# A new order table and new engine choices for a one-core attention and gated feed-forward kernel, with tiles handed out by first release

## The chip, the cores and the metric

The kernel runs on one core of a Trainium2 chip. The metric is the device time of one execution in microseconds (us). A core has five engines with queues of their own: TensorE (PE in the rows; PEld is its weight load), VectorE (DVE), ScalarE (ACT), GpSimd (POOL) and SyncE (SP), which here only issues DMA transfers. Each engine executes its instructions in the order in which they were written, and an instruction waits until the semaphores that it names are set.

## The reference

Inputs are q, k, v of 4 batches, 8 heads, 768 positions and 64 elements per head, 8 memory keys and values per head, and the weights of the feed-forward block.

```python
# attention: chunks of 32 queries see 16 positions to the left, the chunk, 8 to the right, and 8 memory slots
scores = scale * np.matmul(q_c, k_full.transpose(0, 1, 3, 2))
scores = scores - np.max(scores, axis=-1, keepdims=True)
a = np.exp(scores)
a = a / (np.sum(a, axis=-1, keepdims=True) + 1e-09)
out[:, :, c_start:c_end] = np.matmul(a, v_full)
# feed-forward: x is the attention output, 512 wide
h = np.maximum(x @ w_in, 0.0)                   # 512 -> 1024
for k in range(3):
    conv_out += conv_w[k] * hp[:, k:k + S, :]   # along the positions, per channel
gate = 1.0 / (1.0 + np.exp(-conv_out))
out = (h * gate) @ w_out                        # 1024 -> 512
```

## The kernel before, in words

**Attention.** The 4 batches are cut into halves (hf) of 384 positions and head pairs (cc, 4 of them), which makes 32 steps. A step's score matmuls (L310, tile `s`, in PSUM, one buffer) are reduced to their maximum on VectorE (L267), which is subtracted on VectorE and put through exp on ScalarE (L269, L270) or taken as the bias of exp on ScalarE (L283). The result stands in one of two tiles `e0`, `e1`; VectorE sums it (L290) and takes the reciprocal (L293), and VectorE or GpSimd multiplies by it (L294). TensorE transposes the tile (L325, PSUM tile `t`, one buffer), ScalarE copies it out (L327, `w_t`), TensorE multiplies by the values (L334, into the same `t`), and the result is split into a high and a low part, `x_hi` on ScalarE (L340) and `x_lo` on VectorE (L341). The first four steps are done singly, the others in pairs, so that there are 18 groups, named below by their number.

**Feed-forward.** Every product is three matmuls: high by high, high by low, low by high. `w_in` and `w_out` arrive as 64-bit numbers in 16 loads of 512 KB (L208), 8 for each, and are split on the engines into a high and a low part (L212 to L238). The letter of `W_IN` and `W_OUT` says which engines do it for each of the 8 slices: C and M use a copy on ScalarE (L219) and a product (L230, L232); R and S use an addition on GpSimd (L234), a cast on ScalarE (L236) and a subtraction on GpSimd (L238). A small letter puts one step, L214, on GpSimd. `conv_w` (24 KB) arrives in the same buffer as the last slice of `w_in` (L210). `ffn_in` (L358) makes 12 matmuls for a slice fc of the 1024 hidden channels and a half of a batch, three for each head pair; `relu` (L366), the three-tap convolution (L374 or L376, then L378 twice), the sigmoid (L379), the product (L381) and the split into `g` high and low (L387, L388) follow; `ffn_out` (L402) makes 24 matmuls for 128 positions, then a copy (L405) and a store (L406).

**The order.** Nothing is scheduled at build time. Every piece of work is put into a list by `plan.op` (L111) with what it reads and writes; `Plan.run` (L143) then emits the pieces in the order of the table `ORDER`, which therefore sets the order of the instructions on each engine and of the transfers in SyncE's queue. The strings `TAP`, `MULT`, `LO`, `SOFT`, `NORM` choose an engine for one instruction of each group or slice (A ScalarE, V VectorE, G GpSimd; in `SOFT`, A and B are the two forms without the subtraction). A tile belongs to a ring with a fixed number of buffers: four for the loads of weights (`w64`), two for `k_t`, three for `q_d` and `v_t`, four PSUM banks `f`, one `s`, one `t`. A load whose ring has no free buffer waits in SyncE's queue, and all that stands behind it waits too.

The lines of the changed kernel are three to five higher than those of the rows below: L310 became L314, L325 L329, L334 L338, L358 L362, L341 L345, L208 L213, L301 L305, L234 L239, L236 L241, L219 L224, L283 L287, L405 L409.

## Time and profile before

| what | us |
|---|---|
| median of 3 runs | 352.35 (352.2 to 353.53) |
| profiled execution, whole time | 352.37 |
| its span, first to last instruction | 350.6 |
| whole time less span | 1.77 |
| TensorE busy in the span | 334.1 (95%) |
| VectorE, ScalarE, GpSimd busy | 233.1, 191.9, 83.6 |

The profiled execution is within 0.02 us of the median. "Busy" is the union of an engine's instructions. A row of a timeline gives the start, the time from the first start to the last end of a run of like instructions, the engine, line and operation, the tiles as output<-input, and how long the engine had been idle before, with what ended the idle time.

### The profile page before, as it was taken

The numbers are of one execution on the slowest core, as the hardware profiler recorded it, in microseconds if no ns is written. First come the engines' busy times: TensorE is split into PE (matmuls) and PEld (weight loads), VectorE is DVE, ScalarE is ACT, GpSimd is POOL, SyncE is SP. The second block draws the span as 40 slices with busy tenths as digits, with TensorE's granted clock in tenths as the row PEclk, the third lists the DMA queues.
The fourth block names the chain that finished last, engine by engine and source line by source line (L and its number), as shares of the span: only waits on it lengthen the run. The fifth ranks groups of instructions, "written<-read, shape, count | busy, mean of one in ns | idle before, by whom it ended". The sixth has DMA issues, their size and how long they took to land.

```text
span 350.6 us, 10290 instructions
## 1 busy us (share of the span) xinstructions
PE 334.1 (95%) x4536; PEld 297.1 (85%) x4536; DVE 233.1 (66%) x325; ACT 191.9 (55%) x314; POOL 83.6 (24%) x127
## 2 busy tenths in 40 slices
PE   1589999999999999999999999999999999999996
PEld 0468999989999998887888999998888988998885
DVE  4977998999989997989974143286840332678300
ACT  4434785877687869379842323456743352545311
POOL 1464245124473154111020000402200012121200
PEclk9999999999999999999999999999999999999999
DMA  7966979667677244022401600001212000100022
GB/s 261 391 216 204 314 249 333 230 208 228 200 206 251 66 154 148 27 93 75 125 20 36 243 0 32 0 2 60 65 45 93 30 1 2 60 0 2 0 105 76
DMA packets 19916, 42.49 MB, mean 121 GB/s; under 512 B 2336, under 2 KB 10784, under 8 KB 19872
## 3 DMA queue, kind: packets, MB, share of 16 engines
q1 hardware_dynamic: 19872, 41.85, 35.6%
q8 instruction: 35, 0.57, 0.7%
q14 instruction: 9, 0.07, 0.1%
HBM read 35.55 MB, written 6.29 MB: 119 GB/s over the span
## 4 chain that ended last, share of the span: by engine, by line
PE 85%; DVE 9%; DMA 3%; issue 1%; ACT 0%; POOL 0%; DVEq 0%; ACTq 0%; POOLq 0%
PE f L402 38%; PE f L358 34%; PE t L334 6%; PE s L310 4%; PE t L325 3%; DMA w<-in_w_out_dram 2%; DVE c L378 1%; DMA w<-in_w_in_dram 1%; DVE w_top L217 1%; DVE e L269 1%; DVE top L267 1%; DVE w_top L214 1%; DVE w L223 1%; DVE w_top L216 1%; DVE w L221 1%
## 5 line engine op out<-in xcount | busy, mean ns | idle before, releaser
L402 PE MATMUL f<-w_out_hi,g 128*128 128x512 f32 (+1 forms) x400 | 127.3, 387 | 0.0
L358 PE MATMUL f<-x_hi,w_in_hi 128*128 128x384 f32 x256 | 90.3, 353 | 0.0
L402 PEld LDWEIGHTS f<-w_out_hi,g 128*128 128x128 f32 x400 | 74.1, 188 | 15.2 <-ACT o_sb L405 0.2
L358 PE MATMUL f<-x_lo,w_in_hi 128*128 128x384 f32 x256 | 86.7, 339 | 0.0
L358 PE MATMUL f<-x_hi,w_in_lo 128*128 128x384 f32 x256 | 86.7, 339 | 0.0
L402 PE MATMUL f<-w_out_lo,g 128*128 128x512 f32 (+1 forms) x200 | 77.0, 385 | 0.0
L378 DVE SCALAR_TENSOR_TENSOR c<-h,cw,c 128x768 f32<-128x768 f32 x48 | 49.2, 1044 | 18.6 <-ACT c L374 17.4
L358 PEld LDWEIGHTS f<-x_hi,w_in_hi 128*128 128x128 f32 x256 | 48.6, 190 | 2.7 <-issue 0.2
L358 PEld LDWEIGHTS f<-x_hi,w_in_lo 128*128 128x128 f32 x256 | 48.8, 190 | 1.0
L358 PEld LDWEIGHTS f<-x_lo,w_in_hi 128*128 128x128 f32 x256 | 48.5, 190 | 0.0
L402 PEld LDWEIGHTS f<-w_out_lo,g 128*128 128x128 f32 x200 | 37.6, 188 | 6.6
L405 ACT COPY o_sb<-f 128x512 f32<-128x512 f32 (+1 forms) x25 | 14.2, 573 | 43.4 <-PE f L402 41.3
L379 ACT ACTIVATE c<-c 128x768 f32<-128x768 f32 x32 | 26.9, 847 | 19.6 <-DVE c L378 19.5
L366 ACT ACTIVATE h<-f 128x384 f32<-128x384 f32 x48 | 22.6, 490 | 26.3 <-PE f L358 26.3
L388 POOL TENSOR_TENSOR g<-c,g 128x768 fp32r<-128x768 f32 x8 | 15.4, 1925 | 70.9 <-PE f L402 35.2
L334 PEld LDWEIGHTS t<-w_t,v_t 64*64 64x64 f32 x1536 | 25.2, 140 | 4.6 <-issue 3.3
L334 PE MATMUL t<-w_t,v_t 64*64 64x32 f32 x1536 | 27.2, 224 | 0.1
L387 ACT CAST g<-c 128x768 fp32r<-128x768 f32 x24 | 19.8, 833 | 12.6 <-POOL c L381 7.1
L376 DVE TENSOR_SCALAR c<-h,cw 128x768 f32<-128x768 f32 x14 | 8.6, 617 | 26.3 <-ACT h L366 23.6
L388 DVE TENSOR_TENSOR g<-c,g 128x768 fp32r<-128x768 f32 x16 | 17.3, 1086 | 11.2 <-ACT g L387 11.0
L381 POOL TENSOR_TENSOR c<-c,h 128x768 f32<-128x768 f32 x5 | 8.9, 1781 | 63.4 <-ACT c L379 63.4
L341 DVE TENSOR_TENSOR x_lo<-t,x_hi 128x768 fp32r<-128x768 f32 (+1 forms) x18 | 15.5, 859 | 12.6 <-ACT x_hi L340 12.6
(68 smaller groups left out, 408.5 us busy)
## 6 DMA issues: line engine op xcount, KB each, us to landing
v_t<-in_v_dram SPq DMA_DIRECT2D x32, 384.0 KB, 4.4
k_t<-in_k_dram SPq DMA_DIRECT2D x28, 252.0 KB, 3.9
out_dram<-o_sb SPq DMA_DIRECT2D x23, 256.0 KB, 2.0
q_d<-in_q_dram SPq DMA_DIRECT2D x28, 192.0 KB, 4.4
w<-in_w_in_dram SPq DMA_DIRECT2D x8, 512.0 KB, 6.2
w<-in_w_out_dram SPq DMA_DIRECT2D x8, 512.0 KB, 5.3
h<-in_k_dram SPq DMA_DIRECT2D x4, 252.0 KB, 6.1
h<-in_q_dram SPq DMA_DIRECT2D x4, 192.0 KB, 5.8
```

Of the source, the lines that this page charges most:

```text
L310: nc.tensor.matmul(s.t[w * CH:(w + 1) * CH, h ^ w & 1, (i * NG + g) * KW:(i * NG + g + 1) * KW], lhsT=q_d.t[r, c], rhs=k_t.t[r, c * STEP:c ...
L325: nc.tensor.transpose(out=t.t[:, j, g * P:(g + 1) * P], in_=e.t[:, i, 1:1 + 2 * KW], identity=ident)
L334: nc.tensor.matmul(t.t[h * D:(h + 1) * D, c & 1, c // 2 * CH:(c // 2 + 1) * CH], lhsT=vs[i].t[r, o], rhs=w_t.t[r, i, o], start=True, stop= ...
L341: plan.op(lambda: nc.vector.tensor_tensor(out=lo(), in0=sums(), in1=hi().bitcast(F32), op=ALU.subtract), (t, *keys(x_hi)), keys(x_lo))
L358: nc.tensor.matmul(f.t[:, :TW], lhsT=w_in_p[c][:, fc, cc], rhs=x_p[a].t[:, cc], start=cc == 0 and i == 0, stop=cc == NCC - 1 and i == 2)
L366: nc.scalar.activation(h.t[:, 1 + o:1 + o + TW], f.t[:, :TW], AF.Relu)
L378: plan.op(lambda i=i: nc.vector.scalar_tensor_tensor(out=c.t, in0=h.t[:, i:i + S], scalar=w[i], in1=c.t, op0=ALU.mult, op1=ALU.add), (*H, ...
L379: plan.op(lambda: nc.scalar.activation(c.t, c.t, AF.Sigmoid), (c,), (c,))
L387: plan.op(lambda: nc.scalar.copy(out=g_hi(), in_=x()), (h,), (p[0],))
L388: plan.op(lambda: (nc.vector if lo == 'V' else nc.gpsimd).tensor_tensor(out=g_lo(), in0=x(), in1=g_hi().bitcast(F32), op=ALU.subtract), (h ...
L402: nc.tensor.matmul(ps.t[:, :n], lhsT=g[fc][a].t[:, tt * P:(tt + 1) * P], rhs=w_out_p[c][:, fc, o:o + n], start=fc == 0 and i == 0, stop=fc ...
L405: plan.op(lambda: nc.scalar.copy(out=o_sb.t[:, :n], in_=ps.t[:, :n]), (ps,), (o_sb,))
```

## The change

All numbers of `ORDER` are new, and most of the strings of engine choices differ in a few letters. `Plan.run` no longer demands that the tile handed out longest ago is free: it demands that some tile of the ring is free (`left` counts the readers that a tile still has). The tiles `e0` and `e1`, which were handed out in turn, are now kept in a list from which the one released first is taken.

```diff
-W_IN, W_OUT = ('CSSRMSCr', 'CMCRRSRM')
-TAP = 'AAAAAAAAVAVAVVVAVAVAVVAAVVAAVVAV'
-MULT = 'VVVGVVGVVVVVGGGVGVVVVGVVVGGGVVVV'
-LO = 'VVVVGGGVVVVVVVVVGVVVGVVVVGVVGVGV'
-SOFT = 'VVVVVAAVVAVBVVVBVBVVVAVVVVAVVBAA'
-NORM = 'GGVGGGVVGGGGGVGGVVGGVVVVVVVGVGVG'
+W_IN, W_OUT = ('CrSRMSCs', 'CCMSMRRM')
+TAP = 'AAVAAAAAAVAAAAAAVAVAVAVVAAAVVVVV'
+MULT = 'VGGVVGVVVVVGVVVVGVVVVVVGVGVVGGVV'
+LO = 'VVVGGVVVVGVVGVGGVGVGVVVVGVGVVVGV'
+SOFT = 'VVVVVAAVVAVBVVVBVBVVAAVVVVAVBBVA'
+NORM = 'GGGVGGGVVGGGGVGGVVGGGVVVVVVGVGGG'
...
 ORDER = (
-    64, 65, 1, 0, 3, 75, 17, 16, 85, 70, 33, 32, 66, 67, 18, 68, 69, 2, 71, 72, 73, 74, 4, 76, 190, 49, 5, 6, 19, 77,
...
+    64, 0, 1, 75, 49, 17, 16, 70, 65, 32, 71, 86, 33, 66, 73, 67, 68, 72, 2, 3, 74, 4, 48, 76, 5, 194, 77, 6, 139, 81,
...
-        self.rings, self.parts = ({}, defaultdict(list))
+        self.rings, self.parts, self.freed = ({}, defaultdict(list), {})
...
-                    assert len(used) < size or not used[-size].left, i
+                    assert sum((y.left > 0 for y in used)) < size, i
...
             do()
+            for x in tiles:
+                if not x.left and x.ring in self.freed:
+                    self.freed[x.ring].append(x.t)
...
+    plan.ring('e', len(e_of))
+    plan.freed['e'] = e_of
...
-        plan.ring('e', len(e_of))
-        e = Tile('e', lambda: e_of[len(plan.rings['e'][1]) % len(e_of)])
+        e = Tile('e', lambda: plan.freed['e'].pop(0))
```

TensorE near the start of the program, before: the transposes of the second group (`t_276`), the scores of the fourth (`s_285`), the values of the second, three feed-forward matmuls of slice 0 (`f_346`), and the scores of the fifth group in two halves (`s_359`).

```order
L325 MATMUL t_276<-ident_66,e1_73 128x128 x3
L310 MATMUL s_285<-h_144,h_183 32x64 x24
L334 MATMUL t_276<-w_t_311,v_t_128 64x32 x24
L358 MATMUL f_346<-x_hi0_270,w_in_hi_75 128x384
L358 MATMUL f_346<-x_hi0_270,w_in_lo_76 128x384
L358 MATMUL f_346<-x_lo0_273,w_in_hi_75 128x384
L310 MATMUL s_359<-k_t_234,q_d_181 32x64 x24
L310 MATMUL s_359<-k_t_187,q_d_142 32x64 x24
L358 MATMUL f_411<-x_hi0_270,w_in_hi_75 128x384
```

And now, from the same transposes on:

```order
L329 MATMUL t_276<-ident_66,e1_73 128x128 x3
L362 MATMUL f_283<-x_hi0_269,w_in_hi_75 128x384
L362 MATMUL f_283<-x_hi0_269,w_in_lo_76 128x384
L362 MATMUL f_283<-x_lo0_273,w_in_hi_75 128x384
L314 MATMUL s_296<-h_88,h_139 32x64 x24
L338 MATMUL t_276<-w_t_291,v_t_232 64x32 x24
L314 MATMUL s_354<-k_t_193,q_d_144 32x64 x24
L314 MATMUL s_354<-k_t_198,q_d_154 32x64 x24
L329 MATMUL t_419<-ident_66,e0_71 128x128 x3
```

The same six blocks stand between the transposes `t_276` and the end of the fifth group's scores; the three feed-forward matmuls moved from fourth to first place among those behind the transposes.

SyncE's queue, before, from its twelfth to its twenty-third load (`w64` is a slice of `w_in`, or `conv_w`):

```order
L301 DMA q_d_142<-in_q_dram 128x384
L301 DMA h_144<-in_k_dram 128x504
L301 DMA q_d_181<-in_q_dram 128x384
L301 DMA h_183<-in_q_dram 128x384
L301 DMA q_d_185<-in_q_dram 128x384
L301 DMA k_t_187<-in_k_dram 128x504
L208 DMA w64_228<-in_w_in_dram 128x1024
L301 DMA k_t_234<-in_k_dram 128x504
L301 DMA v_t_263<-in_v_dram 128x768
L301 DMA v_t_350<-in_v_dram 128x768
L208 DMA w64_353<-in_w_in_dram 128x1024
L301 DMA k_t_415<-in_k_dram 128x504
```

And now:

```order
L305 DMA h_139<-in_q_dram 128x384
L305 DMA q_d_144<-in_q_dram 128x384
L215 DMA w64_148<-in_conv_w_dram 128x48
L305 DMA q_d_154<-in_q_dram 128x384
L305 DMA q_d_183<-in_q_dram 128x384
L305 DMA k_t_193<-in_k_dram 128x504
L305 DMA k_t_198<-in_k_dram 128x504
L305 DMA v_t_232<-in_v_dram 128x768
L213 DMA w64_261<-in_w_in_dram 128x1024
L213 DMA w64_281<-in_w_in_dram 128x1024
L305 DMA v_t_288<-in_v_dram 128x768
L213 DMA w64_379<-in_w_in_dram 128x1024
```

The load of `conv_w` stands here now and takes one of the four `w64` buffers (it stood just behind the last row shown of before). Ahead of the fifth slice of `w_in` (`w64_353` before, `w64_281` now) stand two loads of values now, where there were four; the numbers of q, k and weight loads ahead of it are the same.

ScalarE around the slice fc4 of `w_in` (before `w_top_443`), before:

```order
L340 CAST x_hi0_270<-t_535 128x384
L283 ACTIVATE e1_73<-s_486,top_595 128x64 x12
L366 ACTIVATE g_639<-f_617 128x384
L219 CAST w_in_hi_75<-w_top_443 128x512
L366 ACTIVATE g_660<-f_346 128x384
```

And now (`w_top_505` is slice fc5, `w_top_562` slice fc4):

```order
L344 CAST x_hi0_269<-t_531 128x384
L287 ACTIVATE e1_73<-s_480,top_601 128x64 x12
L331 COPY w_t_644<-t_628 128x768
L241 CAST w_in_hi_75<-w_top_505 128x512
L370 ACTIVATE g_766<-f_594 128x384
L224 CAST w_in_hi_75<-w_top_562 128x512
```

The cast of fc4 stands behind a copy of `t` and the cast of fc5, which waits for GpSimd's addition on `w_top_505`.

## Rows read from the trace of the kernel before

**Rows 1.** The page's first part: busy time of each engine, share of the span, instructions.

```profile
PE 334.1 (95%) x4536; PEld 297.1 (85%) x4536; DVE 233.1 (66%) x325; ACT 191.9 (55%) x314; POOL 83.6 (24%) x127
```

**Rows 2.** Busy time of each engine by stretches of the span: stretch, its length, then for each engine busy us and instructions, the granted clock, the DMA engines' share and GB/s.

```profile
0.00:16.83 16.83, 5.23 (x195) 4.13 (x195) 11.47 (x28) 7.42 (x12) 4.82 (x13) 1.00 0.90 323
16.83:24.04 7.21, 5.70 (x151) 4.27 (x151) 6.36 (x14) 3.13 (x6) 4.19 (x3) 1.00 0.67 245
...
30.00:72.00 42.00, 41.76 (x992) 38.46 (x990) 39.05 (x68) 29.38 (x57) 16.77 (x28) 1.00 0.78 258
72.00:347.45 275.45, 275.41 (x3092) 244.83 (x3090) 173.26 (x213) 149.95 (x235) 54.71 (x81) 1.00 0.25 83
347.45:350.60 3.15, 0.00 (x0) 0.00 (x0) 0.00 (x0) 0.37 (x1) 0.00 (x0) 1.00 0.14 48
```

**Rows 3.** The three longest waits of TensorE: engine, tile and line, what ended the wait, us in total, times, the longest.

```profile
PE s L310 <- DMA h<-in_q_dram: 8.3, 2, 6.8
PE t L325 <- POOL e L294: 3.2, 2, 1.6
PE s L310 <- issue: 1.5, 1, 1.5
```

**Rows 4.** Timeline of TensorE from 16.8 to 29.7 us, without some of the single f matmuls.

```profile
16.83 0.91 PE L325 MATMUL t<-ident,e 128*128 128x128 f32 x3 [1.55 <-POOL e L294]
17.67 1.27 PE L310 MATMUL s<-h 64*32 64x64 f32 x48
18.87 1.50 PE L334 MATMUL t<-w_t,v_t 64*64 64x32 f32 x48
20.30 0.69 PE L358 MATMUL f<-x_hi,w_in_hi 128*128 128x384 f32 x1
...
21.56 0.97 PE L310 MATMUL s<-k_t,q_d 64*32 64x64 f32 x48
24.04 0.96 PE L310 MATMUL s<-k_t,q_d 64*32 64x64 f32 x48 [1.51 <-issue]
...
27.33 0.52 PE L358 MATMUL f<-x_lo,w_in_hi 128*128 128x384 f32 x1
...
28.14 0.34 PE L358 MATMUL f<-x_lo,w_in_hi 128*128 128x384 f32 x1
```

**Rows 5.** DMA from 16.0 to 21.5 us: packets and rate.

```profile
DMA packets 707, 1.98 MB, mean 360 GB/s; under 512 B 84, under 2 KB 234, under 8 KB 707
```

**Rows 6.** DMA from 21.6 to 22.75 us, by queue: packets, MB, share. The queue q8 brings instructions.

```profile
q8 instruction: 1, 0.02, 5.9%
```

**Rows 7.** The page's part on loads: how many, KB each, median us from issue to landing.

```profile
v_t<-in_v_dram SPq DMA_DIRECT2D x32, 384.0 KB, 4.4
k_t<-in_k_dram SPq DMA_DIRECT2D x28, 252.0 KB, 3.9
...
w<-in_w_in_dram SPq DMA_DIRECT2D x8, 512.0 KB, 6.2
```

**Rows 8.** The two `k_t` loads issued between 11 and 20 us: the view of that tile, from issue to landing.

```profile
L301 SPq DMA_DIRECT2D k_t<-in_k_dram x2: 328/328/328, 11.7 to 13.7; - x2
DMA to landing us min/median/max: 6.1/6.2/6.3
```

**Rows 9.** Timeline of VectorE, single rows between 16 and 39 us.

```profile
16.06 0.56 DVE L341 TENSOR_TENSOR x_lo<-t,x_hi 128x384 fp32r<-128x384 f32 x1
...
36.55 0.69 DVE L217 SCALAR_TENSOR_TENSOR w_top<-w,w_top 128x512 uint32<-128x512 uint32 x1
37.27 0.43 DVE L224 TENSOR_SCALAR w<-w_top 128x512 uint32<-128x512 uint32 x1
37.61 0.69 DVE L217 SCALAR_TENSOR_TENSOR w_top<-w,w_top 128x512 uint32<-128x512 uint32 x1
```

**Rows 10.** Timeline of ScalarE and of GpSimd, single rows between 35 and 41 us.

```profile
35.41 2.56 ACT L283 ACTIVATE e<-s,top 128x64 f32<-128x64 f32 x12
37.77 0.57 ACT L366 ACTIVATE g<-f 128x384 f32<-128x384 f32 x1
38.33 0.62 ACT L219 CAST w_in_hi<-w_top 128x512 fp32r<-128x512 f32 x1
40.47 1.30 POOL L234 TENSOR_TENSOR w_top<-w_top,w 128x512 f32<-128x512 f32 x1 [5.47 <-issue]
```

**Rows 11.** Timeline of TensorE: the first matmul of slice fc4, and the values of the fifth group, which follow the four head pairs of that slice.

```profile
40.45 0.44 PE L358 MATMUL f<-x_hi,w_in_hi 128*128 128x384 f32 x1
...
42.73 1.60 PE L334 MATMUL t<-w_t,v_t 64*64 64x32 f32 x96
```

**Rows 12.** Timeline of TensorE: its one wait behind 30 us, at the transposes of the eighth group.

```profile
71.33 0.85 PE L325 MATMUL t<-ident,e 128*128 128x128 f32 x6 [0.24 <-DVE x_lo L341]
```

**Rows 13.** Timeline of the last 5 us: ScalarE's last two copies and SyncE's last two stores.

```profile
345.35 0.59 ACT L405 COPY o_sb<-f 128x512 f32<-128x512 f32 x1 [2.06 <-PE f L402]
345.96 2.25 SPq L406 DMA_DIRECT2D out_dram<-o_sb  x2
347.49 0.37 ACT L405 COPY o_sb<-f 128x256 f32<-128x256 f32 x1 [1.55 <-PE f L402]
```

**Rows 14.** Timeline of VectorE: the same subtraction twice, at 316 and at 326 us.

```profile
316.50 0.96 DVE L388 TENSOR_TENSOR g<-c,g 128x768 fp32r<-128x768 f32 x1 [1.15 <-ACT g L387]
326.40 1.78 DVE L388 TENSOR_TENSOR g<-c,g 128x768 fp32r<-128x768 f32 x1 [0.90 <-ACT g L387]
```

118 rows, old and new, of the table ORDER are left out of this document.

## The prediction, as put on record before the changed kernel ran

> **What bounds the kernel now.** I read the busy shares first: TensorE is busy 334.1 of 350.6 us, no other engine over 66% [rows 1]. Then I cut the span where TensorE's pace changes [rows 2]: from 30 us to its last matmul at 347.45 it is idle for 0.24 + 0.04 = 0.28 us; its idle time lies in the first 16.83 us (11.6 us), in the next 7.21 us (1.51 us) and behind the last matmul (3.15 us). The matmuls themselves are the same before and after, 3,000 as written, counted in the order. So a new order can gain only idle time, or pace in the first 30 us. The waits name the idle time of the first 30 us [rows 3]: 8.3 us for the first loads, 3.2 us for the first two normalised tiles, and one wait of 1.51 us that is put down to "issue", which is to say to no instruction and no load. The reader is to see it in the timeline [rows 4]: between the two halves of the fifth group's scores TensorE stands from 22.53 to 24.04 us. The operands had long landed: the two k_t loads issued at 11.7 and 13.7 us took at most 6.3 us [rows 8].
>
> **What that wait is.** In just this stretch one packet of the instruction queue arrives, of 0.02 MB [rows 6], where from 16.0 to 21.5 us the loads had the DMA engines to themselves at 360 GB/s [rows 5]. I read it so: TensorE ran out of instructions, since the packet with the next ones stood behind the loads that had been issued before it. The Trainium skill (Runtime: NRT & Kernel Launch, Instruction fetch mechanics) says that a sequencer fetches its next page over its own DMA queue while it executes the one before, so that crossing a page is mostly hidden. By that rule the wait has another cause, which the change doesn't touch, and the sum below would be 1.5 us higher. The trace, with 1.51 us and a packet in it, speaks against the rule at this place.
>
> **The change part by part.**
>
> *The e tiles.* The order shows e0 and e1 in strict turn at all 18 groups, before and after. So this part by itself moves nothing: 0.
>
> *Loads ahead of the instruction packet.* Up to the packet the order before has the loads through v_t_350, and now those through w64_261; the next one, w64_281, waits for GpSimd to release a buffer. It holds two loads of values fewer and conv_w more: 2 x 384 - 24 = 744 KB [rows 7], at 360 GB/s 2.1 us. The packet is then due 2.1 us earlier, and TensorE could go on at 24.04 - 2.1 = 21.9 us. It needs it later. From the transposes at 16.83 us the six blocks take 0.84 (transposes), 1.20 (scores), 1.43 (values), 1.26 (three f matmuls), 0.97 and 0.96 us, each the difference of two starts, or the duration where a wait follows [rows 4]; together 6.66 us, in either order. The second half of the scores is thus reached at 16.83 + 5.70 = 22.5 us, and the wait goes: -1.5 us. Bounds: if w64_281 gets in ahead of the packet after all, 512 KB come back, 1.5 us, and some 0.9 us of the wait stay; if the packet isn't late because of loads, all of it stays. So -1.5 to 0; I take -1.5, since arithmetic leaves 0.6 us to spare.
>
> *The start of this stretch.* The transposes at 16.83 us follow VectorE's x_lo, which ends at 16.62 [rows 9]. The order puts a key load of the fourth group ahead of those of the second: 252 KB at the 323 GB/s of this stretch [rows 2], 0.8 us later for the second and third scores, while GpSimd's first normalisation comes some 0.4 us earlier, as VectorE reaches it without a weight step between. -0.4 to +0.8; the third scores had to wait behind the transposes anyway, and I take 0.
>
> *What must keep up.* A gain of 1.5 us at 25 us holds only if the other engines are 1.5 us earlier too. The tightest place I find is the first matmul of slice fc4, at 40.45 us [rows 11]. Now the fifth group's values, 1.53 us, stand ahead of it, so TensorE comes there at 40.45 - 1.5 + 1.5 = 40.5 us. It needs ScalarE's cast of fc4, which stands behind the cast of fc5, which waits for GpSimd's addition, which waits for VectorE. Stepping along the queues of the new order with durations of the trace, I estimate that VectorE finishes x_lo of the fourth group at 34.1 us (its transposes at 31.0, its values until 32.9, then ScalarE's copy and VectorE's subtraction). Then come seven weight steps, three long and four short: a long and a short one together take 37.61 - 36.55 = 1.06 us, a short one 0.34 [rows 9], so 3.52 us, to 37.6. GpSimd adds in 1.30, to 38.9; ScalarE casts fc5 in 0.62, does a relu in 0.57 and casts fc4 in 0.62 [rows 10]: 40.7 us. The twelve exponentials of 2.56 us [rows 10] start at 33.6 and are out of the way at 36.2. So the cast is ready 0.2 us behind TensorE: +0.2, with nothing to spare. Bounds: 0, and +2.5 if the seven steps run as much slower as the same subtraction did from one place to another, 1.78 us for 0.96 [rows 14]: 3.52 x 0.82 / 0.96 = 3.0 more, of which 0.5 could be made up elsewhere.
>
> *VectorE farther on.* The one wait behind 30 us ends on VectorE [rows 12]. The new choices take off VectorE, counted in the order, two first taps, three subtractions `LO` and two normalisations, and give it one product: with the subtraction's 0.96 us [rows 14] for each, an estimate, some 6 us of its 233 less. Those ahead of the eighth transposes are worth more than 0.24 us, so this wait goes: -0.2; at the other end it stays, 0. GpSimd takes the most of it over, and is busy 24% [rows 1].
>
> *The end.* In the last slices the order leaves about the same distance between the last gate and the matmuls that need it (some 15 us of output matmuls). The last full copy comes nine half-width matmuls, 1.06 us, ahead of the end instead of 18: its 256 KB store then runs beside the last one, which was issued 2 us behind it [rows 13]. Bounds 0 and +0.7 (256 KB at 360 GB/s); I take +0.2.
>
> *The clock.* The granted clock is given as 1.00 throughout [rows 2], but an f matmul takes 0.52 us at 27.33 and 0.34 at 28.14 [rows 4]; I read the first as the lower of the two levels, 1.2 GHz, the second as 2.4. The rise can come earlier, since TensorE works without the gap, or stay at about 27.9. Some nine f matmuls and a block of values now lie between 23.5 and 27.9 at the lower level, as six to nine did: 0, with 9 x (0.52 - 0.34) = -1.6 as the other end (these matmuls at full pace).
>
> Sum: -1.5 + 0 + 0.2 - 0.2 + 0.2 = -1.3 us, from a span of 350.6 to 349.3, and with the 1.77 us around it 351.1 us. That is also what I set against the median, since the profiled execution stands at it.
>
> **The rivals.**
> - *The issue wait stays.* TensorE waits at this place of its program for something that the loads don't set, or w64_281 is sent sooner than I think and the packet is as late as before. For it: the row says "issue" and nothing names the packet as the cause; against it: a packet of the instruction queue arrives in just that wait [rows 6]. Then the span is 350.6 + 0.2 - 0.2 + 0.2 = 350.8, and the time 352.6 us. (The skill's rule on the fetch, above, speaks for this one.)
> - *The clock rises sooner.* Without the gap TensorE is at work from 16.8 us on. For it: the pace rose only after 27.85 - 24.04 = 3.8 us of work behind the gap [rows 4]; against it: 5.70 us of work in the 7.21 us up to the gap's end did not bring it [rows 2]. Then 351.1 - 1.6 = 349.5 us.
> - *The convoy at fc4 becomes the bound.* One mechanism, at 37 to 43 us: ScalarE's cast of fc4 behind that of fc5 behind GpSimd behind VectorE. GpSimd has two normalisations more in this stretch. It decides from 1.5 us of delay on; at 2.5 us it gives 351.1 - 0.2 + 2.5 = 353.4, and with the 0.5 not made up 353.9 us, slower than before.
>
> **How the numbers follow.** A measurement of this kernel can tell some 0.5%, or 1.8 us, from no change: faster is below 350.6, slower above 354.1. My forecast of 351.1 has a chance of 0.42, with its own range of 350.2 to 351.9, a third of it below 350.6; the wait that stays 0.24; the sooner clock 0.18, nearly all faster; the convoy 0.16, of which half above 354.1 (VectorE is held up once more). That gives faster 0.14 + 0.18 + 0.01 = 0.33, slower 0.08, to which I add 0.03 for what I haven't seen, and same 0.56. The range from 349.2 to 353.7 leaves out a fifth: the far ends of the clock and of the convoy.
>
> **What would show it.** In the new profile the wait put down to issue is gone from TensorE's list, or under 0.5 us, and the second half of the fifth scores follows the first at 22.5 us; the first matmul of fc4 starts at 40.7 us; no wait of TensorE behind 30 us is longer than 0.5 us; TensorE's last matmul ends near 346.0. It would be wrong if the issue wait stood there unchanged, or if a wait for ScalarE's w_in_hi or GpSimd's w_in_lo of over 1 us stood at 40 us.

## The result, and the profile after

The changed kernel takes 354.23 us (median of 8 runs, 353.87 to 355.16), the kernel before beside it 352.51 (8 runs, 350.53 to 353.53): a ratio of 1.0064, with a 95% interval of 1.0043 to 1.0084. It is slower by some 0.6%, and above the predicted range. The profiled execution took 354.62 us, with a span of 352.8. (One profile told below, that of before_v_later, is of an execution 4 us longer than its kernel's median; the places of its waits and packets and what follows them are taken from it, not its time.)

The page's first part for the changed kernel answers to [rows 1]; nothing in it has moved by more than 5 us:

```profile
PE 333.5 (95%) x4536; PEld 297.4 (84%) x4536; DVE 234.0 (66%) x321; ACT 196.0 (56%) x344; POOL 88.1 (25%) x129
```

The waits of TensorE, as in [rows 3] (what waits and what ended it, us in total, times, the longest):

```profile
PE s L314 <- DMA h<-in_k_dram: 6.1, 1, 6.1
PE s L314 <- DVE z L294: 3.4, 1, 3.4
PE s L314 <- issue: 2.2, 1, 2.2
PE t L329 <- DVE x_lo L345: 1.7, 1, 1.7
```

The wait put down to issue is still there and is longer, 2.2 us for 1.5. But it is another one. TensorE's timeline at 22 us, where [rows 4] had it, and at 36 us and behind, without most of the single f matmuls:

```profile
21.92 1.23 PE L314 MATMUL s<-k_t,q_d 64*32 64x64 f32 x96 [0.40 <-PE t L338]
23.54 0.55 PE L329 MATMUL t<-ident,e 128*128 128x128 f32 x3 [0.39 <-POOL e L298]
...
24.10 0.34 PE L362 MATMUL f<-x_hi,w_in_lo 128*128 128x384 f32 x1
...
36.62 1.11 PE L314 MATMUL s<-k_t,q_d 64*32 64x64 f32 x86
39.92 0.32 PE L314 MATMUL s<-k_t,q_d 64*32 64x64 f32 x10 [2.19 <-issue]
40.17 1.60 PE L338 MATMUL t<-w_t,v_t 64*64 64x32 f32 x96
41.71 0.67 PE L362 MATMUL f<-x_hi,w_in_hi 128*128 128x384 f32 x1
42.17 0.52 PE L362 MATMUL f<-x_hi,w_in_lo 128*128 128x384 f32 x1
...
45.29 0.33 PE L362 MATMUL f<-x_lo,w_in_hi 128*128 128x384 f32 x1
```

The fifth group's scores now run through without a gap (x96 in one row), and the f matmuls are at 0.34 us from 24.10 us on, where they were at 0.52 until 27.96. Then a later set of scores breaks off after 86 matmuls for 2.19 us, and the f matmuls behind it take 0.52 us again until 45 us. A packet of the instruction queue arrives in that gap too; the DMA view from 37.4 to 38.4 us (queue, packets, MB, share), as in [rows 6]:

```profile
q8 instruction: 1, 0.02, 5.5%
```

The windows, cut at these places, show the fall of pace in the granted clock (stretch, length, busy us of TensorE, its weight loads, VectorE, ScalarE and GpSimd, granted clock, DMA share, GB/s):

```profile
16.83:24.04 7.21, 5.79 (x202) 4.98 (x203) 7.11 (x16) 3.66 (x7) 5.32 (x5) 1.00 0.75 246
24.04:30.00 5.96, 5.48 (x118) 4.73 (x117) 5.29 (x11) 3.01 (x5) 4.56 (x4) 1.00 0.85 283
30.00:37.73 7.73, 7.73 (x214) 6.92 (x212) 7.48 (x15) 4.80 (x16) 2.98 (x3) 1.00 0.95 323
37.73:39.92 2.19, 0.00 (x1) 0.00 (x0) 2.14 (x4) 1.51 (x3) 0.60 (x2) 1.00 0.65 196
39.92:41.71 1.79, 1.79 (x107) 1.65 (x106) 1.29 (x2) 0.00 (x0) 1.79 (x4) 1.00 0.95 341
41.71:45.05 3.34, 3.34 (x16) 3.34 (x11) 2.96 (x6) 3.10 (x5) 1.48 (x4) 0.51 0.94 344
...
349.26:352.80 3.54, 0.00 (x0) 0.00 (x0) 0.00 (x0) 0.37 (x1) 0.00 (x0) 0.94 0.33 113
```

The row at 41.71 reads 0.51, the lower of the two levels. (The row at 16.83 reads 1.00 with f matmuls of 0.52 us in it, as before: there the level is seen in the durations only.)

**The account.** From a span of 350.6 to one of 352.8 us, +2.2, term by term: the second transposes start at 17.46 instead of 16.83, +0.63; the wait at 22.5 is gone, -1.51; three short waits have come, 0.40 and 0.39 (above) and 0.48 for a `k_t` at 27.2, +1.27; the wait at 37.73, +2.19; ten f matmuls at 41.71 to 45.05 that take 3.34 us, where the ten from 40.45 us on took 1.84 in the kernel before, at full pace, +1.50; the wait of [rows 12] is gone, -0.24; the end is 3.54 for 3.15 us, +0.39. That is +4.23; the -2.0 left over is put down to the earlier rise of the pace, at 24.1 for 27.96 us.

### The profile page after: what moved, and what is told of

Read it like the earlier page. It is cut to its first block, busy times and chain, and to the rows that moved or that the text cites. A ratio compares the mean times of both kernels' runs of the same rounds, so it can differ in the third digit from the quotient of the medians.

```text
span 352.8 us, 10320 instructions
## 1 busy us (share of the span) xinstructions
PE 333.5 (95%) x4536; PEld 297.4 (84%) x4536; DVE 234.0 (66%) x321; ACT 196.0 (56%) x344; POOL 88.1 (25%) x129
## 4 chain that ended last, share of the span: by engine, by line
PE 93%; DMA 3%; issue 1%; ACT 1%; DVE 1%; SPq 0%; ACTq 0%; DVEq 0%
PE f L362 39%; PE f L406 38%; PE t L338 7%; PE s L314 5%; PE t L329 3%; DMA w<-in_w_in_dram 2%; DMA k_t<-in_k_dram 1%; ACT w_top L217 0%; ACT e L274 0%; SPq L305 0%; DVE top L271 0%; DVE z L294 0%; DVE e L273 0%; DVE x_lo L345 0%; ACT x_hi L344 0%
## 5 line engine op out<-in xcount | busy, mean ns | idle before, releaser
L382 DVE SCALAR_TENSOR_TENSOR c<-h,cw,c 128x768 f32<-128x768 f32 x48 | 52.9, 1111 | 22.5 <-ACT c L378 21.0
L406 PEld LDWEIGHTS f<-w_out_lo,g 128*128 128x128 f32 x200 | 37.6, 188 | 6.4
L383 ACT ACTIVATE c<-c 128x768 f32<-128x768 f32 x32 | 26.8, 846 | 14.9 <-DVE c L382 14.7
L392 POOL TENSOR_TENSOR g<-c,g 128x768 fp32r<-128x768 f32 x7 | 12.9, 1845 | 59.8 <-ACT g L391 59.8
L338 PE MATMUL t<-w_t,v_t 64*64 64x32 f32 x1536 | 27.3, 224 | 0.2 <-ACT w_t L331 0.2
L385 POOL TENSOR_TENSOR c<-c,h 128x768 f32<-128x768 f32 x5 | 7.8, 1565 | 69.9 <-ACT c L383 69.9
L298 POOL TENSOR_TENSOR e<-e,z 128x768 f32<-128x768 f32 (+1 forms) x11 | 16.3, 1485 | 25.8 <-DVE z L297 23.4
L392 DVE TENSOR_TENSOR g<-c,g 128x768 fp32r<-128x768 f32 x17 | 19.3, 1132 | 3.4 <-ACT g L391 3.1
```

The costliest lines, as they stand in the source:

```text
L298: plan.op(lambda: (nc.vector if norm == 'V' else nc.gpsimd).tensor_tensor(out=keep()[:, :N], in0=keep()[:, :N], in1=z.t[:, :N].unsqueeze(3 ...
L338: nc.tensor.matmul(t.t[h * D:(h + 1) * D, c & 1, c // 2 * CH:(c // 2 + 1) * CH], lhsT=vs[i].t[r, o], rhs=w_t.t[r, i, o], start=True, stop= ...
L382: plan.op(lambda i=i: nc.vector.scalar_tensor_tensor(out=c.t, in0=h.t[:, i:i + S], scalar=w[i], in1=c.t, op0=ALU.mult, op1=ALU.add), (*H, ...
L383: plan.op(lambda: nc.scalar.activation(c.t, c.t, AF.Sigmoid), (c,), (c,))
L392: plan.op(lambda: (nc.vector if lo == 'V' else nc.gpsimd).tensor_tensor(out=g_lo(), in0=x(), in1=g_hi().bitcast(F32), op=ALU.subtract), (h ...
L406: nc.tensor.matmul(ps.t[:, :n], lhsT=g[fc][a].t[:, tt * P:(tt + 1) * P], rhs=w_out_p[c][:, fc, o:o + n], start=fc == 0 and i == 0, stop=fc ...
```

## The experiments

Each was timed beside the kernel before; the last two are single executions. Each run has one profile. In the diffs, the numbers are pieces of work in the order of `ORDER`, named in the text.

### Is the late packet set by the loads ahead of it?

**after_v_behind_w.** A load of values and one of queries go behind a load of weights each.

```diff
 ORDER = ( ...
-    ... 203, 294, 204, ... 62, 192, 218, ...
+    ... 203, 204, ... 62, 218, ... 127, 192, 63, 138, 294, ...
```

(192 and 294 are loads of `v_t` and `q_d`, 127 and 138 those of slices fc6 and fc7.)

> The changed kernel with two loads moved behind weight loads in SyncE's queue: a load of values (384 KB) behind the seventh slice of w_in, which can only be sent at about 32.6 us, and a load of q (192 KB) behind the eighth. Theory (the instruction packet queues behind the loads that were sent before its request, at about 32 us): 576 KB less stand ahead of it, 1.6 us at 360 GB/s, so the packet comes at about 35.9 us instead of 37.44, TensorE's issue wait of 2.19 us at 37.73 shrinks to under 0.7 us, the fall of its pace at 41.7 us goes with it, and the time is 350.5 to 351.5 us instead of 354.2. Rival (the wait belongs to this place of the program, whatever the loads): 2.2 us of wait and 354.2 us. Rival (sharing: the packet competes with all that is under way): the same bytes are sent within a microsecond, no change, 354.2 us.

Measured: 354.74 us, 1.0064 (1.0038 to 1.0090). The wait at 37.4 us was 2.86 and the packet came at 37.96 to 38.94, no earlier. But the load of fc6, which now had no values ahead of it, went out at 31.26 us instead of 32.57, and the values right behind it; both landed before the packet came (35.8 and 37.8 us). So the edit did not take bytes from ahead of the packet, and the run doesn't show what fewer bytes would have done.

**after_w_later.** The loads of fc6, fc7 and the first slice of `w_out` go behind the next loads of keys and queries.

```diff
 ORDER = ( ...
-    ... 166, 127, 63, 138, 113, ... 125, 497, 224, ... 290, 112, ...
+    ... 166, 63, 113, ... 125, 224, ... 290, 127, 138, 497, 112, ...
```

> The changed kernel with the seventh and eighth slice of w_in and the first load of w_out (512 KB each) moved behind a k and a q load. They went out at 32.6, 33.0 and 38.0 us. Theory (queue behind earlier loads): if the packet was behind the seventh slice, it comes up to 1.4 us earlier, 36.0 to 36.8 us, and the issue wait at 37.73 us is 0.7 us or less, with no fall of the pace: 350.5 to 351.5 us; if the request came before that slice was sent, nothing changes, 354.2 us. Rival (place of the program): 2.2 us of wait stay, 354.2 us. The weights would arrive at about 42 to 43 us and are first read at 43.65, so no new wait from them, or under 0.5 us.

Measured: 356.34 us, 1.0128 (1.0096 to 1.0160). The packet came at 32.7 to 33.7 us and there was no issue wait. The weights, though, were now late; TensorE's longest wait, at 45.5 us, and ScalarE's, which it stands behind:

```profile
PE f L362 <- ACT g L370: 2.5, 1, 2.5
...
46.27 1.22 ACT L217 ACTIVATE w_top<-w 128x536 f32<-128x536 f32 x2 [2.88 <-DMA w<-in_w_in_dram]
```

The pace fell behind it (f matmuls of 0.52 us from 50.2 to 51.5 us). Moving the weights past other loads only exchanges the wait. That it is the weights that set the packet, this profile doesn't show by itself: the changed kernel unaltered also got the packet in time twice (after_again, after_again_2 below).

**before_v_later.** The kernel before, with the two loads of values of its old late packet put behind a `k_t`.

```diff
 ORDER = ( ...
-    ... 38, 50, 24, ... 150, 34, 97, ...
+    ... 38, 24, ... 150, 97, ... 211, 34, 50, ...
```

> The kernel before with two loads of values (768 KB) moved behind the fifth slice of w_in and behind the key load that is sent at 22.56 us, so that they aren't under way when the packet for the fifth group's second half is asked for. Theory (queue): the packet comes 2.1 us earlier, at 19.5 us, the issue wait of 1.51 us at 22.53 us goes, and the clock's rise comes sooner too, as in the changed kernel (23.4 instead of 27.9 us): 352.5 - 1.5 - 1.6 = 349.4 us, or 351.0 if the rise doesn't move. Rival (place): wait stays, 352.5 us. Rival (a new wait for the values that come later takes it back): a wait of TensorE for w_t or v_t at 27 us, 351 to 352.5 us.

Measured: 352.96 us, 1.0024 (0.9999 to 1.0049). The wait at 22.5 us was gone, as in the changed kernel. There came 1.7 us for `v_t` at 26.8, and issue waits of 0.95 us at 33.8 and 1.76 at 40.7 us, with a fall of pace behind the latter and none behind the other two. The gain at the first place was lost farther on in this execution too, with the old order.

```profile
26.80 0.90 PE L334 MATMUL t<-w_t,v_t 64*64 64x32 f32 x48 [1.71 <-DMA v_t<-in_v_dram]
27.63 0.44 PE L358 MATMUL f<-x_hi,w_in_hi 128*128 128x384 f32 x1
27.91 0.33 PE L358 MATMUL f<-x_hi,w_in_lo 128*128 128x384 f32 x1
```

**after_page_shift.** If a wait stands where one packet ends and the next isn't there, 128 more instructions ahead must move it to other work.

```diff
+    x = psum.tile([P, 512], F32, name='f', tag='f', bufs=4)
+    for i in range(32):
+        nc.tensor.matmul(x[0:32, 0:64], lhsT=ident[0:64, 0:32], rhs=ident[0:64, 0:64], start=True, stop=True)
```

> The changed kernel with 32 small score-like matmuls of the identity in front of the first score, where TensorE idles for 6 us; they compute nothing that is used. They put 128 more instructions ahead in TensorE's stream, so that every instruction packet ends 128 instructions earlier in the program. Theory (the wait sits where one packet of 256 instructions ends and the next is late): no wait stays at the second half of the scores at 37.7 us; the next packet's end comes at about 34.8 us, its packet is asked for at about 30.6 us, with less under way, and is there by 34.3 us: no wait or under 0.5 us, and 350.5 to 351.5 us. There may be a wait at another end, near 20.6 us. Rival (place of the program): the wait of 2.2 us stays at the same scores, 354.2 us.

Measured: 362.14 us, 1.0286 (1.0257 to 1.0316). The scores that were cut at 37.73 run through, and four other places are cut. Of the 8 us that it takes longer than the changed kernel, these four waits (5.5 us, for 2.2) and two falls of pace are seen; the rest isn't assigned. The timeline:

```profile
41.52 0.88 PE L341 MATMUL t<-w_t,v_t 64*64 64x32 f32 x42 [1.33 <-issue]
...
55.06 0.55 PE L341 MATMUL t<-w_t,v_t 64*64 64x32 f32 x22 [1.52 <-issue]
126.75 0.54 PE L317 MATMUL s<-k_t,q_d 64*32 64x64 f32 x35 [1.24 <-issue]
142.79 0.63 PE L317 MATMUL s<-k_t,q_d 64*32 64x64 f32 x38 [1.36 <-issue]
```

Count TensorE's instructions in the order of their starts, weight loads and the semaphore instructions of its sequencer included. Then the first instruction behind every issue wait of over 0.1 us that ends after 16 us, 22 in the traces of all kernels here, has an index that is 193 more than a multiple of 256. Eight of them (entry: when TensorE began the 256 instructions before):

| kernel | index | mod 256 | entry | packet | wait | resumed behind the packet |
|---|---|---|---|---|---|---|
| before | 705 | 193 | 18.27 | 21.60-22.69 | 1.51 | 1.35 |
| after | 1473 | 193 | 31.76 | 37.44-38.33 | 2.19 | 1.60 |
| after_v_behind_w | 1473 | 193 | 31.28 | 37.96-38.94 | 2.86 | 1.32 |
| after_page_shift | 1729 | 193 | 38.21 | 39.17-40.16 | 1.33 | 1.36 |
| after_page_shift | 5825 | 193 | 139.44 | 140.18-141.49 | 1.36 | 1.30 |
| after_old_choices | 1217 | 193 | 27.63 | 31.85-32.80 | 2.62 | 1.39 |
| before_v_later | 1473 | 193 | 34.72 | 39.93-40.90 | 1.76 | 1.53 |
| before_gated | 1473 | 193 | 31.02 | 36.50-37.51 | 2.03 | 1.50 |

So the wait is a property of the packet's end and not of the work there. The four of after_page_shift show a second way to it: 256 instructions that are nearly all short matmuls are through in 2.0 us, and the packet comes too late though it comes 0.7 to 1.1 us after entry.

### Holding loads back

A gate is a one-element memset of the load's buffer on VectorE, ahead of the load, which then can't be issued before VectorE gets there.

```diff
-        plan.op(lambda: nc.sync.dma_start(out=w.t[:, :n]...
+        plan.op(lambda: (nc.vector.memset(w.t[0:1, 0:1, 0:1].bitcast(F32), 0.0) if key == 'in6' else None, nc.sync.dma_start(out=w.t[:, :n]...
 ORDER = ( ...
-    ... 166, 127, 63, 138, 113, ...
+    ... 166, 63, 113, ... 114, 127, 138, ...
```

**after_w_gate_35** has this gate for slice fc6, with fc7 behind it; **after_w_gate_34** the same two places of VectorE's order earlier.

> The changed kernel with the seventh and eighth slice of w_in held back from 32.6 and 33.0 us to about 35.0 and 35.4 us by a one-element memset on VectorE, which the load has to wait for; what is sent before them is under way until 36.8 us, so the weights should arrive as before, at about 38.6 and 40 us, ahead of their first use at 43.65. Theory (the packet asked for at about 31.5 us waits as long as weight loads follow on closely; with these loads far behind the packet came at 32.71 us): the packet comes between 32.7 and 34.5 us, no issue wait at 37.7 us, no fall of TensorE's pace at 41.7 us; that takes 2.2 + 1.5 us off: 350.5 us, between 350.0 and 351.2. Rival (the packet stands behind every load sent before about 32.3 us): it comes at 36.8 us, the wait is some 1.6 us, the fall stays, 353.5 us. Rival (the wait isn't what costs the time; another engine is the bound behind it): the wait goes, and the time stays at 354.

> The same with the memset 1.3 us earlier, so that the two loads go out at about 33.7 and 34.1 us. Theory: the packet still passes before them, 350.5 us; if it doesn't come before 34 us, then the wait stays at 1.5 to 2.2 us, with 353.5 to 354.2 us. Between the two kernels this tells how far behind the request the weight loads have to be.

Measured: 353.76 us, 1.0037 (1.0017 to 1.0057), and 353.86, 1.0042 (1.0025 to 1.0058). In both profiles the packet for index 1473 was in time, with neither wait nor fall. The loads went out at 38.7 and 36.7 us, later than meant. The gain was small; in both profiles the packet for index 705 was late (waits of 1.37 and 0.46 us at 22 us) and the pace rose only at 32.8 and 31.8 us.

**after_gate_fc4** and **after_both_gates** hold slice fc4 and a load of values back, from 18.0 and 18.4 us to some 19 us, so that the packet for index 705 is in time; the second has the gate for fc6 as well.

```diff
-    ... 84, 107, 150, 39, 34, 91, ...
+    ... 84, 150, 39, 91, ... 40, 107, 34, ...
```

> Only the first of these gates: the fifth slice of w_in and the values behind it at 19.5 us instead of 18. Theory: no wait at 22 us, the rise of the pace at about 24 us as in the profiled run of the changed kernel, the issue wait of some 2.2 us at 37.7 us and the fall at 41.7 us stay: 354.2 us, 353.6 to 354.8; so the price of the second late packet with its fall is the difference between this kernel and the one with both gates, 3.7 us. Rival (the second wait has nothing to do with the weight loads that are sent at 32.6 us): both kernels have it, and the same time.

> The changed kernel with two gates of the same kind: the fifth slice of w_in and the load of values behind it are held back from about 18 to 19.5 us, and the seventh and eighth slice to about 35 us or later. Theory (each late packet costs twice, as a wait and as a time at TensorE's lower pace, and each of the two packets is late only if a weight load gets in ahead of it): the packet of the fifth group's scores is there by 21 us, no issue wait at 22 us, the pace rises at about 24 us, no issue wait at 37 us, no fall behind it: 354.2 - 2.2 - 1.5 = 350.5 us, 349.8 to 351.2, faster than the kernel before. Rival (what the first gate holds back makes the next packet late): a wait of 1 to 2 us at the page end at 27 or 31 us and a fall of the pace, 353 to 354.5 us. Rival (another engine sets the time behind 30 us): waits for VectorE or ScalarE take the gain back, 353 to 354 us.

Measured: 353.34 us, 1.0033 (0.9997 to 1.0070), and 352.68, 1.0010 (0.9973 to 1.0047). With one gate both packets happened to be in time in the profile; the wait expected at 37.7 us wasn't there, so this pair doesn't price the second packet. With both, the whole of TensorE's waits behind 17.5 us is:

```profile
PE t L329 <- DVE x_lo L345: 0.5, 1, 0.5
PE f L362 <- POOL w_in_lo L243: 0.3, 1, 0.3
PE s L314 <- PE t L338: 0.2, 1, 0.2
```

No issue wait and no fall is left. By the ratios, 0.54 of the 0.64% that the change cost are back (by the medians of the changed kernel and this one, 1.5 us); with six executions, anything from 0.1 to 1.0% fits. The kernel is then about level with before, not faster. The first of the waits, at 34 us, is none that the prediction had: the fifth group's transposes wait until VectorE has read the one tile `t`. The second, at 43.3 us, is for GpSimd's low part of slice fc5, behind the convoy of the prediction.

Over all profiles but that of after_page_shift: with fc4 held back, the packet for index 705 ended at 19.3 to 20.1 us (five profiles), without at 20.2 to 22.7 us (ten; before_v_later, 20.3, not counted). So this packet does come earlier when the load is out of its way. For index 1473 the two overlap: with fc6 or fc7 sent later or held back, it ended 1.9 to 4.7 us after TensorE began the block before (six profiles), without 2.1 to 7.7 us (ten). No wait stands there in the six, nor in six of the ten.

**after_gates_cover_tail** also puts two blocks of f matmuls ahead of the transposes that wait for `x_lo`, and reorders the last output matmuls.

```diff
-    ... 109, 205, 122, 114, 163, 110, 167, ... 1302, 1285, 1303, 1286, 1304, 1305, 1287, ...
+    ... 109, 163, 167, 205, ... 1256, 1285, 1297, ... 1257, 1286, 1287, 1300, ...
```

> The changed kernel with both gates and two edits of TensorE's order: two of the feed-forward matmul triples that stood behind the fifth group's transposes go ahead of them (they cover the 0.50 us for which TensorE waited for x_lo at 33 us), and the last matmuls of the last but one output tile with their copy and 256 KB store go ahead of the last half tile, so that the store doesn't run beside the last one. Theory (with the packets in time, what is left of the loss is these two: 0.5 us and 0.44 us): 352.7 - 0.9 = 351.8 us, 351.2 to 352.3, and a time behind the last matmul of 3.2 us instead of 3.63. Rival (the next wait or a late packet takes it back): 352.3 to 353.5 us.

Measured: 353.18 us, 1.0027 (1.0005 to 1.0049). The end fell from 3.6 to 3.19 us as expected. But the wait for `x_lo` only moved, to the f matmuls behind (0.40 us), and the median shows no gain. Four of the twelve executions have a mean granted clock of 0.990 to 0.995 and take 354.2 to 358.4 us, as if TensorE's pace had fallen in them: the gates don't spare every execution that.

### Order and choices apart

**after_old_choices** is the new order with the old strings `TAP`, `MULT`, `LO` and `NORM`, **before_new_choices** the old order with the new ones; `W_IN`, `W_OUT` and `SOFT` stay with the order.

```diff
-TAP = 'AAVAAAAAAVAAAAAAVAVAVAVVAAAVVVVV'
+TAP = 'AAAAAAAAVAVAVVVAVAVAVVAAVVAAVVAV'
...
```

> The changed kernel's order with the old strings TAP, MULT, LO and NORM (W_IN, W_OUT and SOFT, which change the number of steps, stay new). About 6 us of work go back from GpSimd and ScalarE to VectorE. Theory (TensorE is the bound behind 30 us, the engine choices matter only where it waits): 354.2 us, within 0.5, with a wait for VectorE of some 0.2 to 0.5 us more at 71 us. Rival (the order needs the new choices): waits of TensorE for VectorE between 60 and 130 us, over 1 us in sum, 355 us or more.

> The kernel before with the new strings TAP, MULT, LO and NORM in the old order. The new order with the old strings was 6 us slower than with the new ones, through a late packet at 31 us and waits for weights and gates between 144 and 182 us. Theory (order and choices fit only together): new waits of TensorE for GpSimd or ScalarE, 353.5 to 357 us. Rival (the new choices are better or the same in any order, since VectorE has less to do): 351.5 to 352.8 us, and the 0.24 us of wait at 71 us gone.

Measured: 360.46 us, 1.0231 (1.0205 to 1.0256), and 362.79, 1.0282 (1.0255 to 1.0310). Each half alone costs 2 to 3%. In the first, the longest wait is one for a packet, 2.62 us (index 1217 in the table), with a fall of pace behind it. In the second, TensorE waits for engines where the kernel before did not; that each of these has a step more there than the order leaves time for is a reading, not shown:

```profile
PE f L358 <- ACT h L366: 2.6, 2, 2.3
...
PE t L325 <- DVE x_lo L341: 1.1, 1, 1.1
PE f L402 <- ACT g L387: 0.9, 1, 0.9
```

The two parts can't be priced one by one; they fit only each other. (The third part, the e tiles, moves nothing: with the tiles handed out in turn, the changed kernel's instructions stand in the same order on every engine. It wasn't run.)

### The same gates on the kernel before

**before_gated** holds slice fc4 and two loads of values of the kernel before back from 14 to 16 us to 19.4 to 20.4 us. **before_two_gates** also holds slice fc7 and the two loads of values behind it back.

```diff
-    ... 38, 50, 24, ... 150, 34, 97, 106, 98, ...
+    ... 38, 24, ... 42, 106, 34, 50, 91, ... 150, 97, 98, ...
...
-    ... 126, 192, 152, ... 275, 196, 118, 219, 63, 220, 137, ...
+    ... 126, 152, ... 275, 118, 219, 137, 192, 196, 63, 220, ...
```

(The first pair of lines is in both, the second in before_two_gates alone.)

> The kernel before, its order of work unchanged, with the three loads that stand ahead of its late packet (the fifth slice of w_in and two loads of values, 1,280 KB) held back from 14 to 16 us until about 19.2 us, by a one-element memset on VectorE. What is sent before them has landed by 19.8 us; the values are first read at 28.4 us. Theory (the packet of the fifth group's second half waits only for what was sent ahead of its request, and one late packet costs a wait and a late rise of the pace): it comes at 19.8 us, the issue wait of 1.51 us at 22.5 goes, the pace rises at about 24.5 us instead of 27.9, and if no later packet is late, the time is 352.4 - 1.5 - 1.0 = 349.9 us, faster than both kernels. Rival (TensorE, 2.5 us earlier, meets the packets at 31 and 38 us late, as it did when these values were loaded later): issue waits of 0.5 to 1.8 us there, a fall of the pace behind them, 352 to 353.5 us.

> The kernel before with the first gate as in before_gated, and a second one: the fc7 slice of w_in, which the kernel before issues at about 31 us, and the two value loads that stand behind it in SyncE's queue are held back until a one-element memset on VectorE behind the fourth group's maximum, at about 32.4 us. The computation is unchanged. Theory of the next late packet: in before_gated TensorE's instruction packet for index 1473, asked for at about 31.0 us, came at 36.5 to 37.5 us, needed at 37.0; with these loads held back it is in by 35 us, TensorE has no wait put down to issue of over 0.4 us at 36 to 38 us, no fall of pace behind it at 39 to 43 us, and all executions lie in the lower half of before_gated's (349.5 to 350.8, median 350). Rival, that the packet isn't set by these loads: it is as late as before, the issue wait of 2 us and the fall stay, and the time is 352 to 353.5. Second rival, that the loads held back are then late themselves: TensorE waits for the fc7 weights or for v_t between 36 and 48 us by over 0.5 us, 351.5 to 353.

Measured for before_gated: 352.35 us, 0.9998 (0.9965 to 1.0031). The wait at 22.5 us is gone, the pace rises at 23.0 us, and the changed kernel's second wait has come, in a kernel that has the old order:

```profile
35.90 1.08 PE L310 MATMUL s<-k_t,q_d 64*32 64x64 f32 x83
39.01 0.34 PE L310 MATMUL s<-k_t,q_d 64*32 64x64 f32 x13 [2.03 <-issue]
39.27 0.69 PE L358 MATMUL f<-x_hi,w_in_hi 128*128 128x384 f32 x1
39.76 0.52 PE L358 MATMUL f<-x_hi,w_in_lo 128*128 128x384 f32 x1
```

Its twelve executions fall into two groups by the mean granted clock that each shows: six with 0.990 to 0.995 take 352.99 to 354.49 us, six with 0.998 to 1.000 take 349.86 to 351.72.

Measured for before_two_gates: 350.86 us, 0.9959 (0.9928 to 0.9990), 0.4% faster than the kernel before, and by the two ratios some 1% faster than the changed one. In its profile the scores of 37 us are whole and the pace behind them is the full one:

```profile
36.92 1.24 PE L310 MATMUL s<-k_t,q_d 64*32 64x64 f32 x96
38.09 0.45 PE L358 MATMUL f<-x_hi,w_in_hi 128*128 128x384 f32 x1
38.38 0.33 PE L358 MATMUL f<-x_hi,w_in_lo 128*128 128x384 f32 x1
```

Behind 17.5 us TensorE waits for nothing until its last matmul; the window up to there:

```profile
72.00:344.86 272.86, 272.86 (x3025) 242.67 (x3017) 170.49 (x209) 148.22 (x233) 54.70 (x81) 1.00 0.24 81
```

Of twelve executions one shows a granted clock under 0.998 (six did with one gate). The expectation that all lie at 349.5 to 350.8 was too narrow: six do; 351.2 and 351.3 lie just above, and 352.3, 352.4, 353.9 (all with a clock of 1.000) and 355.0 well above. What held those up no profile shows.

### Two more executions of the changed kernel

**after_again** and **after_again_2** are the changed kernel unaltered. In five of its eight timed executions the mean granted clock is 0.998 to 1.000, so they had no fall like that of the profiled one, whose mean is 0.995, and yet they take as long.

> The changed kernel as it is, looked at once more: in five of its eight timed executions the mean granted clock is 0.998 to 1.000, so that no fall of 3 us at 42 us can have taken place there, and yet they take 353.9 to 355.2 us, as long as the profiled one with the fall. Theory that late packets cost them too, in another form: an execution without the fall has an issue wait at index 705 (22 us) with the pace rising only at 28 to 33 us, or a wait at index 1473 (38 us) over 2 us, and the sum of issue waits and of the time at the lower pace behind 18 us is the same within 1 us as in the profiled one. Rival: such an execution has packets in time at both places and loses its time in waits for weights or x_lo of over 1.5 us together.

> The changed kernel as it is, a third look, since one look may show the execution with the fall again. Expected as for after_again: either the fall at 42 us behind an issue wait of 2 us or, with a granted clock of 0.998 and more, an issue wait at 22 us and a late rise of pace; rival as there.

Measured: 352.86 and 353.23 us, with granted clocks of 0.999 and 1.000 (one execution of before beside them: 353.19). In the first, TensorE's timeline at 22 us and at 38 us:

```profile
22.55 0.96 PE L314 MATMUL s<-k_t,q_d 64*32 64x64 f32 x48 [0.47 <-issue]
...
38.08 1.20 PE L314 MATMUL s<-k_t,q_d 64*32 64x64 f32 x96
39.21 1.60 PE L338 MATMUL t<-w_t,v_t 64*64 64x32 f32 x96
40.74 0.45 PE L362 MATMUL f<-x_hi,w_in_hi 128*128 128x384 f32 x1
```

The packet for index 1473 came at 34.5 to 35.4 us here, some 2.9 us earlier than in the profiled execution of the same kernel, and the wait and the fall are not there. In after_again_2 it came at 33.1 to 34.1 us. The packet's time is thus not fixed by the order of the loads; it varies from run to run. In after_again the gain went to a late rise (27.3 us), 0.47 us of issue wait, 0.8 for `x_lo`, 0.3 each at two other places, and the longer end: TensorE's last matmul ends at 347.5 us, where it ended before. Neither the sum expected (the same loss in another form) nor the rival (1.5 us of waits for weights or `x_lo`) was found. These two executions are 0.6 us and more below the eight timed ones, so they do not show what those five lost.

## Why the prediction was wrong, point by point

*That wait is an instruction packet, and fewer loads ahead of it bring it earlier.* Right. Forecast was 2.1 us earlier; the packet ended at 20.59 instead of 22.69 us in the profiled execution, 2.1 us, and the wait of 1.51 us went. The second half of the scores followed the first. That the size fits to the tenth is luck: in after_again and after_again_2 the same packet ended at 21.08 and 21.35 us, and in before_new_choices, with the loads of before, at 21.64. That loads set it is shown by the five profiles with fc4 held back. The rule of the Trainium skill (Runtime: NRT & Kernel Launch, Instruction fetch mechanics), that the next block of 256 instructions is fetched while the one before runs, agrees with the index of all 22 waits. That the cost of crossing a block is "mostly hidden", as it also says, these traces contradict wherever 256 instructions pass in about 2 us, or the packet comes late behind loads: waits of up to 2.9 us of TensorE's time. The bound, that the next weight slice gets in ahead and 0.9 us of the wait stay, is what happened in after_again: that slice landed at 20.77 us, before the packet's end, and 0.47 us of wait stayed. It was 0.14 us in after_again_2, and 0.4 to 1.4 in three kernels with the same start.

*What must keep up.* Here the prediction failed. "A gain of 1.5 us at 25 us holds only if the other engines are 1.5 us earlier too" asks for the engines, and only for them. The next instruction packets have to keep up as well: in the profiled execution the one for index 1473 arrives at 38.33 us, and TensorE, which is early, stands for 2.19 us. The step priced a packet once, at the place where the old trace showed a wait, and took the loads as the cause without asking where the next of the 35 packets meets the loads. It also had no price for what follows a wait: the fall of pace, 1.50 us. Both together, +3.7 us, are more than the forecast's error for this execution (352.8 against 349.3, 3.5).

For the median the cause is shown in part only. Three of the eight timed executions have the lower mean clock of such a fall (0.994 to 0.995) and take 354.06 to 354.81 us; the five without it take 353.87 to 355.16, no less, and none of the five was profiled. That both gates bring back most of the loss speaks for late packets in them too, but it is a difference of medians with a wide interval, and the packet for index 1473 was also in time in three profiles where nothing held a load back for it (after_again, after_again_2, after_gate_fc4).

*The convoy at fc4.* In the profiled execution its terms were too late by 0.8 to 1.2 us, on the safe side: VectorE's `x_lo` ended at 33.3 (forecast 34.1) and its seven weight steps at 36.6 (37.6); ScalarE's cast of fc4 ended at 39.5 (40.7). In after_again, where no packet held TensorE up there, they ended at 35.1, 38.3 and 41.3, too early by 0.6 to 1.0. There the first matmul of fc4 started at 41.38 us (the three from 40.74 on are of fc0), right behind the cast, and the second at 41.73, right behind VectorE's low part of fc4 (41.68). So the place is as tight as forecast and costs 0.2 us there, with 0.27 more for fc5 at 44.1; the rival "convoy", though the time came out near its 353.9, is not what happened.

*VectorE farther on.* Right in place: the transposes of [rows 12] start without a wait now. But the reason given, some 6 us less on VectorE, did not come about: it is busy 234.0 us for 233.1, with four instructions fewer, since like ones ran longer (48 convolution steps 52.9 us, before 49.2).

```profile
71.41 0.82 PE L329 MATMUL t<-ident,e 128*128 128x128 f32 x6
```

*The start of this stretch.* Taken as 0 with bounds of -0.4 and +0.8: it was +0.63 in the profiled execution and -0.18 in after_again (16.65 us).

*The end.* +0.2 forecast, +0.39 measured, within the bounds. The reason given is the right one: the 256 KB store goes out 0.85 us ahead of the last one, which then takes 2.1 us to land, where it took 1.7.

```profile
348.22 0.59 ACT L409 COPY o_sb<-f 128x512 f32<-128x512 f32 x1 [2.37 <-PE f L406]
348.84 1.19 SPq L410 DMA_DIRECT2D out_dram<-o_sb  x2
```

*The clock.* The rival "the clock rises sooner" came true at 24.1 us, at about -2.0 us for a forecast bound of -1.6, and the pace was lost again at 41.71. That the lower level could return was in no case. The rival "the issue wait stays" was wrong as it was put, since the wait at its place went and the packet is its cause, but an issue wait at a later packet has the same effect and is larger than the 1.5 us that it was given.

*What stays open.* With neither packet late the changed kernel has a median of 352.68 us and the kernel before one of 350.86. Of the 2.4 us between their two profiles (350.4 and 348.0), 0.3 lie ahead of the second transposes and 1.4 in idle time behind (0.23 at 21.1 us, 0.50 `x_lo`, 0.26 `w_in_lo`, 0.44 the end); 0.7 is spread and not assigned. Why a packet begins up to 4.4 us before TensorE enters the block ahead of it at one time, and 6.7 us after at another, isn't settled: loads in flight delay it, but nothing here shows when it is asked for. And what the changed kernel's five executions without a fall lost was not seen.

## What to carry to other kernels

A wait put down to issue is best read with the instruction's index: if it is at the end of a block of 256, look at every later block that TensorE will reach sooner once the first wait is gone, and at the loads in flight there. A gain of 1.5 us early in the program can be worth nothing if a later packet, or the next load, doesn't come earlier too. A large load can be kept out of a packet's way by a gate on a cheap instruction; with two of them the old order of work was 0.4% faster than without, while a shift of loads moved the wait to the weights or to later packets. And a packet's time varies between executions, so one profile doesn't tell whether it is in time in the others.

## What the runs showed of the hardware that was not expected

- TensorE stops at instruction indices 256 apart and at no other when an instruction packet is late: 22 of 22 issue waits. It goes on 1.2 to 1.6 us after the packet is in; and in none of the 17 profiles does it begin a block less than 1.2 us after that block's packet, wait or not.
- A block of 256 short instructions, 2.0 us long, was followed by a wait of 1.2 to 1.5 us in all four cases of after_page_shift, even at 126 and 142 us, though the packet began within 1.1 us of entry: from entry to the next block's start took 3.2 to 3.6 us.
- Behind waits of 1.33 us (at 42 us), 1.52, 1.76, 2.03, 2.19, 2.25 (at 104 us), 2.46, 2.62 and 2.86 us the f matmuls went from 0.34 to 0.52 us and came back to 0.34 within a few us; behind waits of 0.82, 0.95, 1.24 and 1.36 us (the last two at 126 and 142 us), and of 1.71 us at 25.1 us in before_v_later, they stayed at 0.34. So the length of the wait alone doesn't decide it. The fall of the profiled execution cost 1.50 us, beside a wait of 2.19.
- The same program, run again, gets the same packet at 34.1, 35.4 or 38.3 us.
